# A chunked linear-attention and Mish feed-forward kernel: scores ahead of outputs in the head, three q chunks loaded in runs of eight rows, transposes and loads of the third group moved

## The chip, the cores and the metric

The kernel runs on one core of one Trainium2 chip. The metric is the device time of one execution in microseconds (us). The core has five engines with instruction queues of their own: TensorE (PE in the profile, with its weight loads as PEld), VectorE (DVE), ScalarE (ACT), GpSimd (POOL) and SyncE (SP). DMA transfers are issued from the queues of ACT, POOL and SP, and move through 16 DMA engines.

## The reference, cut to what matters

```python
# q, k, v: 4 batches, 8 heads, 768 positions, 64 columns; lam: one decay per head
Dmask = where(i >= j, lam ** (i - j), 0)
for each block of 64 positions:
    intra = ((qb @ kb.T) * Dmask) @ vb
    inter = (qb * lam ** (i + 1)) @ kv_state
    out[block] = intra + inter
    kv_state = lam ** 64 * kv_state + (kb * lam ** (63 - i)).T @ vb
x = out as 3072 tokens x 512
h = x @ w_in                                   # 512 x 2048
y = (h * tanh(softplus(h))) @ w_out            # 2048 x 512
```

## The kernel before, in words

**Tiles.** The kernel takes blocks of 128 positions (C) in place of 64, so there are 6 groups (n) of 4 batches (b), 24 chunks c = 4n + b. A chunk is one tile of q, of k and of v: 128 positions by 8 heads by 64 columns. Chunk 0 of q and k comes as float32 over the SP and ACT queues; everything else is loaded by `load_k`, `load_q` and `load_v` (lines 62 to 79) from POOL's queue, which turns float32 into float16 on the way. `chunk_rows` (line 58) puts a position on a partition, so that each of a chunk's 1024 runs is one row of 64 float32.

**The first two groups (chunks 0 to 7)** are turned with TensorE. `first_t` (line 205) transposes k and q against the identity into PSUM tiles pk and pq, four matmuls each, and copies them to SBUF as pkT (on ACT, line 219) and pqT (on DVE, line 222, or line 224 with the decays lq for chunks 4 to 7). `first_s` (line 227) makes the scores, eight matmuls into two PSUM tiles pS, and masks them on DVE into the two tiles sb (line 238; for chunks 0 to 3 the mask dm holds the decays). `first_o` (line 241) makes the outputs: eight matmuls of sb and v into pO (line 253), for chunks 4 to 7 also four of pqT and the state wst (line 249), and a copy to xt on ACT (line 255). `busy(m)` (line 163) issues m matmuls on zeros whose result nobody reads.

**State.** `scale_k` (line 260) multiplies k with its decays into ktil, on DVE for chunks 0 to 3 and 20 to 23 and on POOL for the others. `state_half` (line 281) makes half of a group's new state: 32 small matmuls pv of ktil and v (line 288), then on DVE wst (line 295, group 0) or raws (lines 301 and 303), from which POOL makes wc (line 304). `clear(b)` sets a part of wst to zero on DVE.

**Later groups.** `turn` (line 267) scales k and transposes q and k by DMA from SP's queue into qraw and kraw (line 272). `pair_s`, `pair_o` and `pair_a` work on two chunks at once: scores and state part (lines 324 and 330), outputs (line 351), state (line 288). Their output xtok goes to xt by a DMA transpose from SP (line 361).

**Dense part.** `mm1_unit` (16 for a group) and `mm1_tile` (16 for group 1) make h: ph = w_in times xt (lines 380 and 398), then Mish on ACT into hsg (lines 387 and 402). `mm2_unit` makes the result: po = hsg times w_out (line 412), copied by ACT (line 427) and stored.

**What sets the order.** Nothing is scheduled by the compiler: every engine runs its instructions in the order in which the kernel's lines issue them. The head is lines 451 to 485. Then come the loads of group 1 and of w_out on POOL's queue, the 16 units of group 0 with steps hung on unit numbers by the table `steps` (line 506), the 16 tiles of group 1 with a second table (line 524), the loads and turns of group 2 (line 533), and from line 537 the loop over the later groups, where pair steps are hung on positions of the dense list (line 553).

Of the kernel before, what the change touches and what calls it, by code (L numbers as in the profile page):

```python
# [7 lines left out]
F32 = mybir.dt.float32  # L8
F16 = mybir.dt.float16
# [11 lines left out]
def kernel(  # L21
# [39 lines left out]

    def load_k(i):
        if i == 0:
            kn[i] = const.tile([128, H, D], F32, name="kn0")
            nc.sync.dma_start(out=kn[i], in_=chunk_rows(k, i))
            return
        kn[i] = loads.tile([128, H, D], F16, name="kn", tag="kn")
        nc.gpsimd.dma_start(out=kn[i], in_=chunk_rows(k, i))  # L68

    def load_q(i):  # L70
        if i == 0:
            qn[i] = const.tile([128, H, D], F32, name="qn0")
            nc.scalar.dma_start(out=qn[i], in_=chunk_rows(q, i))
            return
# [122 lines left out]

    xt = [None] * NG
# [6 lines left out]
    def first_t(c, m=0):  # L205

        out_ = []
        first = c < B
        for src, name in ((k0 if c == 0 else kn[c] if first else ktil[c], "pk"),
                          (q0 if c == 0 else qn[c], "pq")):  # L210
# [6 lines left out]
            out_.append(work.tile([128, JP, C], F16, name=f"{name}T", tag=f"{name}T", bufs=2))  # L217
            if name == "pk":
                nc.scalar.activation(out_[-1], pt, AF.Copy)
                busy(m)  # L220
            elif first:
                nc.vector.tensor_copy(out_[-1], pt)
            else:
                nc.vector.tensor_tensor(out=out_[-1], in0=pt, in1=lq, op=ALU.mult)
        kq[c] = out_

    def first_s(c):

        kT, qT = kq[c]
# [5 lines left out]
        sb0[c] = []  # L235
        for t in range(2):
            sb0[c].append(work.tile([128, JP, C], F16, name="sb", tag="sb", bufs=4))
            nc.vector.tensor_tensor(out=sb0[c][t], in0=pS[t],  # L238
                                    in1=dm[:, t] if c < B else bc(maskT, 1, JP), op=ALU.mult)

    def first_o(c):
# [5 lines left out]
        for j in range(JP):  # L247
            if n:
                nc.tensor.matmul(psO[:, j, :], wst[:, b, j, :],
                                 kq[c][1][:, j, :], start=True, stop=False)  # L250
# [4 lines left out]
        nc.scalar.activation(xt[n][:, :, b * C : (b + 1) * C], psO, AF.Copy)  # L255
# [201 lines left out]
    first_t(0, 2)  # L457
# [5 lines left out]
    busy(1)  # L463
    first_s(0)
    first_t(1)
    clear(1)
    q_decays()
    busy(1)
    first_o(0)
    first_s(1)  # L470
    busy(3)
    first_t(2)
    clear(2)
    nc.scalar.preload_act_table(AF.Mish)
    first_o(1)
    first_s(2)
    busy(3)
    first_t(3)
    clear(3)
# [7 lines left out]
    scale_k(1)  # L487
    for i in range(B, NVB - 2):
        load_chunk(i)
# [3 lines left out]
    load_v(NVB - 2)  # L493
    load_k(NVB - 1)
    scale_k(B + 1)
# [10 lines left out]
    steps = {12: ((first_t, 4),), 14: ((first_s, 4),), 15: ((first_t, 5), (first_o, 4))}  # L506
    for u in range(NKI):
# [3 lines left out]
        if u == 1:  # L511
            scale_k(2)
            scale_k(3)
# [7 lines left out]
    c = 2 * B  # L521
    for f, i in ((load_k, c + 1), (load_q, c + 1), (load_k, c + 2), (load_q, c + 2)):
        f(i)
    steps = {(4, 0): ((first_s, 5), (first_t, 6)), (4, 1): ((first_o, 5), (first_s, 6)),
             (4, 2): ((first_t, 7),), (4, 3): ((first_o, 6), (first_s, 7)), (5, 0): ((first_o, 7),),
             (6, 1): ((state_half, 0),), (6, 2): ((state_half, 1),)}
# [5 lines left out]
    c = 2 * B  # L532
    for f, i in ((load_k, c + 3), (load_q, c + 3), (turn, c), (turn, c + 1), (load_v, c),
                 (turn, c + 2), (load_v, c + 1), (turn, c + 3), (load_v, c + 2), (load_v, c + 3)):
        f(i)

    for n in range(NT - 1, NG):
# [9 lines left out]
        if n + 1 < NG:  # L547
# [5 lines left out]
            steps = (((11, pair_s, 0), (14, pair_o, 0), (17, pair_s, 1), (20, pair_o, 1),  # L553
# [60 lines left out]
```

## Time and profile before

| | us |
|---|---|
| median of 3 runs (212.65, 213.41, 213.62) | 213.41 |
| the profiled execution, its own time | 213.85 |
| its span, first to last instruction | 212.1 |
| PE busy | 203.5 |
| POOL busy | 100.0 |
| ACT busy | 86.7 |
| DVE busy | 67.6 |
| packets of POOL's DMA queue, share of 16 engines' span | 85.2% |

In the profile a row of the timeline has the start and the length in us, then the engine, the line of the kernel, the operation, the tiles (written <- read) with shapes, and the number of instructions merged in the row; in brackets stands the idle time of the engine ahead of it and what ended it. A row's length runs to the end of its last instruction, and matmuls overlap, so the next row may start earlier. The list of waits gives for an engine and a line the idle time in all, how often, and the longest. The chain of waits is the sequence of work that ended last, each piece with its start and length. The mean granted TensorE clock is 0.999 over the span.

### The profile page before, as it was taken

The numbers are of one execution on the slowest core, as the hardware profiler recorded it, in microseconds if no ns is written. First come the engines' busy times: TensorE is split into PE (matmuls) and PEld (weight loads), VectorE is DVE, ScalarE is ACT, GpSimd is POOL, SyncE is SP. The second block draws the span as 40 slices with busy tenths as digits, with TensorE's granted clock in tenths as the row PEclk, the third lists the DMA queues.
The fourth block names the chain that finished last, engine by engine and source line by source line (L and its number), as shares of the span: only waits on it lengthen the run. The fifth ranks groups of instructions, "written<-read, shape, count | busy, mean of one in ns | idle before, by whom it ended". The sixth has DMA issues, their size and how long they took to land.

```text
span 212.1 us, 4293 instructions
## 1 busy us (share of the span) xinstructions
PE 203.5 (96%) x1758; PEld 110.5 (52%) x1758; DVE 67.6 (32%) x124; ACT 86.7 (41%) x150; POOL 100.0 (47%) x143
## 2 busy tenths in 40 slices
PE   7989898999999899999999999999999999999994
PEld 4655446999745454445554454544444544444442
DVE  7686613725004442042440042482042510000000
ACT  4764575655421112346412356312456321566120
POOL 7997389932996348786965067921000000000000
PEclk9999999999999999999999999999999999999999
DMA  9999999999999999999997799997702032100112
GB/s 129 133 157 185 189 156 99 172 189 164 121 145 195 185 182 164 163 189 153 156 166 148 182 87 84 144 166 141 190 9 49 5 99 104 49 0 0 49 53 99
DMA packets 109895, 26.78 MB, mean 126 GB/s; under 512 B 102578, under 2 KB 106930, under 8 KB 109874
## 3 DMA queue, kind: packets, MB, share of 16 engines
q0 software_dynamic: 78080, 13.37, 85.2%
q1 hardware_dynamic: 27296, 6.63, 20.4%
q10 hardware_dynamic: 4498, 6.49, 9.9%
q8 instruction: 14, 0.23, 0.5%
q14 instruction: 7, 0.06, 0.1%
HBM read 27.26 MB, written 6.29 MB: 158 GB/s over the span
## 4 chain that ended last, share of the span: by engine, by line
PE 82%; DMA 9%; DVE 2%; ACT 1%; POOL 1%; issue 1%; SPq 1%; POOLq 0%; ACTq 0%; DVEq 0%
PE po L412 33%; PE ph L380 30%; DMA kraw<-ktil 7%; PE ph L398 7%; PE pO L253 2%; PE pS L324 2%; DMA kn<-in_k_dram 2%; PE pO L351 2%; PE pS L234 1%; PE pv L288 1%; PE pk L213 1%; SPq L272 1%; PE busy L167 1%; PE pq L213 1%; POOL vz L79 1%
## 5 line engine op out<-in xcount | busy, mean ns | idle before, releaser
L412 PE MATMUL po<-wout,hsg 128*128 128x512 f16 (+2 forms) x400 | 85.4, 371 | 0.0
L380 PE MATMUL ph<-xt,win 128*128 128x512 f16 (+2 forms) x328 | 73.0, 374 | 0.5 <-ACT xt L255 0.3
L387 ACT ACTIVATE hsg<-ph 128x512 f16<-128x512 f32 x80 | 47.7, 597 | 31.4 <-PE ph L380 31.1
L412 PEld LDWEIGHTS <-hsg 128*128 128x128 f16 x400 | 37.8, 98 | 42.3
L380 PEld LDWEIGHTS <-win 128*128 128x128 f16 x328 | 30.9, 98 | 36.3 <-issue 2.0
L427 ACT ACTIVATE osb<-po 128x512 f32<-128x512 f32 (+1 forms) x24 | 14.2, 593 | 74.8 <-PE po L412 69.9
L339 DVE TENSOR_TENSOR sb<-pS,maskT 128x512 f16<-128x512 f32 x32 | 19.9, 684 | 59.6 <-PE pS L324 59.6
L68 POOL DMA_DIRECT2D kn<-in_k_dram x23 | 21.0, 913 | 4.5 <-issue 1.9
L76 POOL DMA_DIRECT2D qn<-in_q_dram x23 | 20.9, 907 | 4.6 <-DMA wout<-in_moe_w_out_dram 3.0
L79 POOL DMA_DIRECT2D vz<-in_v_dram x24 | 21.7, 908 | 2.4 <-DMA win<-in_moe_w_in_dram 1.6
L263 POOL TENSOR_TENSOR ktil<-kn,lk 128x512 f16<-128x512 f16 x16 | 16.7, 1054 | 2.5 <-DMA kn<-in_k_dram 2.3
L398 PE MATMUL ph<-xt,win 128*128 128x128 f16 x256 | 15.6, 219 | 0.7 <-ACT xt L255 0.7
L357 DVE TENSOR_TENSOR xtok<-pO,lqt 128x512 f16<-128x512 f32 x16 | 10.3, 687 | 15.5 <-PE pO L351 15.5
L398 PEld LDWEIGHTS <-win 128*128 128x128 f16 x256 | 14.5, 98 | 1.1 <-issue 0.8
L304 POOL TENSOR_TENSOR wc<-raws,lbc 128x512 f16<-128x512 f32 x8 | 8.6, 1096 | 9.8 <-DVE raws L303 5.4
L402 ACT ACTIVATE hsg<-ph 128x512 f16<-128x512 f32 x16 | 9.6, 597 | 7.5 <-PE ph L398 7.5
L421 DVE COPY osb<-po 128x128 f32<-128x128 f32 x1 | 0.3, 291 | 38.7 <-PE po L412 38.7
L368 POOL COPY tick<-hsg 1x1 f16<-1x1 f16 x25 | 4.4, 178 | 12.5 <-ACT hsg L387 12.4
L167 PE MATMUL busy<-kzero 128*128 128x512 f16 x16 | 6.6, 505 | 1.2 <-DVE kzero L149 1.2
L253 PE MATMUL pO<-sb,vz 128*128 128x128 f16 x64 | 6.4, 230 | 0.4 <-DVE sb L238 0.3
L238 DVE TENSOR_TENSOR sb<-pS,maskT 128x512 f16<-128x512 f32 x8 | 5.2, 687 | 5.1 <-PE pS L234 5.1
L263 DVE TENSOR_TENSOR ktil<-kn,lk 128x512 f16<-128x512 f16 (+1 forms) x8 | 6.5, 849 | 0.0
(71 smaller groups left out, 115.9 us busy)
## 6 DMA issues: line engine op xcount, KB each, us to landing
out_dram<-osb ACTq DMA_DIRECT2D x23, 256.0 KB, 2.6
vz<-in_v_dram POOLq DMA_DIRECT2D x24, 128.0 KB, 4.4
kn<-in_k_dram POOLq DMA_DIRECT2D x23, 128.0 KB, 5.2
qn<-in_q_dram POOLq DMA_DIRECT2D x23, 128.0 KB, 4.8
wout<-in_moe_w_out_dram POOLq DMA_DIRECT2D x4, 512.0 KB, 10.4
win<-in_moe_w_in_dram POOLq DMA_DIRECT2D x3, 512.0 KB, 9.9
kn<-in_k_dram SPq DMA_DIRECT2D x1, 256.0 KB, 3.4
qn<-in_q_dram ACTq DMA_DIRECT2D x1, 256.0 KB, 4.1
```

What stands on the lines that cost most here:

```text
L68: nc.gpsimd.dma_start(out=kn[i], in_=chunk_rows(k, i))
L76: nc.gpsimd.dma_start(out=qn[i], in_=chunk_rows(q, i))
L79: nc.gpsimd.dma_start(out=vz[i % NVB][:, :, 0:D], in_=chunk_rows(v, i))
L253: nc.tensor.matmul(psO[:, j, :], vf[:, o : o + 128], sb0[c][t][:, j, :], start=(n == 0 and t == 0), stop=(t == 1))
L263: (nc.vector if i < B or i >= (NG - 1) * B else nc.gpsimd).tensor_tensor(out=t, in0=kn[i], in1=bc(lk, 2, D), op=ALU.mult)
L339: nc.vector.tensor_tensor(out=s.sb[x][t], in0=pS[x][t], in1=bc(maskT, 1, JP), op=ALU.mult)
L357: nc.vector.tensor_tensor(out=xtok[:, :, :, t, :], in0=s.pO[t], in1=bc(bc(lqj[:, :, t], 1, 2), 3, D), op=ALU.mult)
L380: nc.tensor.matmul(ph_t[ni][:, lo:hi], win_t(ni, kc), xt[n][:, kc, lo:hi], start=(kc == 0), stop=(kc == NKC - 1))
L387: nc.scalar.activation(hsg[n][:, ni, :], ph_t.pop(ni), AF.Mish)
L398: nc.tensor.matmul(ph[:, u, :], win_t(w * s + u, kc), xt[n][:, kc, b * C : (b + 1) * C], start=(kc == 0), stop=(kc == NKC - 1),)
L412: nc.tensor.matmul(po[:, lo:hi], hsg[n][:, ki, b * C : (b + 1) * C], wout[part][:, kk, lo:hi], start=(ki == 0), stop=(ki == NKI - 1),)
L427: nc.scalar.activation(o, i, AF.Copy)
```

## The change

Five things change.

1. q of chunks 1 to 3 is loaded with eight successive rows of one head on a partition: 128 runs of 2 KB in place of 1024 of 256 bytes. Partition 16h + s then holds rows 8s to 8s + 7 of head h. `turn_pe` turns such a tile with 16 matmuls in place of 4: for each of the eight rows r and for even and odd heads, the weights are the 64 columns of row r, the moving operand is the 64 columns of the identity that pick the heads of that parity, and the result goes to every eighth float32 column of 64 partitions of pq. That tile is float32 where it was float16.
2. In the head, scores stand ahead of outputs, and the two masks of a chunk are split, so that the q copy of the next chunk stands between them. The fillers are dealt out anew (16 before and after), the clears move, and `q_decays` and the load of the Mish table move ahead.
3. `scale_k` of chunks 2 and 3 moves from behind the first half state to the end of the head, and `clear(3)` with it. On POOL `scale_k(5)` moves ahead of the load of k of chunk 7.
4. In the group 0 and group 1 parts the tables shift: chunk 4 is turned after unit 11 (was 12), scored after 13 (was 14); chunk 5 is turned after 14 (was 15) and scored after 15 (was after tile (4,0)); the outputs of chunk 7 come after tile (5,1) (was (5,0)).
5. k and q of chunk 11 are loaded ahead of the state of group 1, and chunk 8 is turned between the two halves of that state. In the loop for group 2 the pair steps stand at 9, 13, 16 and 20 (were 11, 14, 17 and 20).

```diff
     def load_q(i):
...
+        if i < B:
+            qn[i] = const.tile([128, RS, D], F16, name=f"qn{i}")
+            n, b = divmod(i, B)
+            nc.gpsimd.dma_start(
+                out=qn[i].rearrange("p r c -> p (r c)"),
+                in_=q[b, :, n * C : (n + 1) * C, :].rearrange("h (s r) c -> h s (r c)", r=RS))
             return
...
+    own = ident.rearrange("p (j x s) -> p j x s", j=JP, x=2)
...
+    def turn_pe(c, name):
+
+        src = (k0 if c == 0 else kn[c] if c < B else ktil[c]) if name == "pk" else (q0 if c == 0 else qn[c])
+        if 0 < c < B and name == "pq":
+            pt = ps.tile([128, JP, C], F32, name=name, tag=name)
+            for r in range(RS):
+                for x in range(2):
+                    nc.tensor.matmul(
+                        pt[64 * x : 64 * x + 64].rearrange("p j (s r) -> p j s r", r=RS)[:, :, :, r],
+                        src[:, r, :], own[:, :, x, :], start=True, stop=True)
+        else:
             pt = ps.tile([128, JP, C], F16, name=name, tag=name)
...
-    first_t(0, 2)
+    first_k(0)
+    busy(2)
+    first_q(0)
     clear(0)
...
-    busy(1)
-    first_s(0)
-    first_t(1)
-    clear(1)
     q_decays()
     busy(1)
-    first_o(0)
-    first_s(1)
-    busy(3)
+    scores(0)
+    masks(0, 0)
+    first_t(1)
+    masks(0, 1)
+    nc.scalar.preload_act_table(AF.Mish)
+    busy(1)
+    scores(1)
+    masks(1, 0)
+    outputs(0)
     first_t(2)
+    copy_out(0)
+    masks(1, 1)
+    busy(2)
+    first_s(2)
+    first_o(1)
+    clear(1)
+    busy(2)
+    first_t(3)
     clear(2)
-    nc.scalar.preload_act_table(AF.Mish)
-    first_o(1)
-    first_s(2)
-    busy(3)
-    first_t(3)
-    clear(3)
+    busy(2)
     first_s(3)
     first_o(2)
     busy(2)
...
     scale_k(0)
     scale_k(1)
+    clear(3)
+    scale_k(2)
+    scale_k(3)
...
-    steps = {12: ((first_t, 4),), 14: ((first_s, 4),), 15: ((first_t, 5), (first_o, 4))}
+    steps = {11: ((first_t, 4),), 13: ((first_s, 4),), 14: ((first_t, 5),), 15: ((first_o, 4), (first_s, 5))}
...
-    c = 2 * B
-    for f, i in ((load_k, c + 1), (load_q, c + 1), (load_k, c + 2), (load_q, c + 2)):
-        f(i)
+    g = 2 * B
+    for c in (g + 1, g + 2, g + 3):
+        load_k(c)
+        load_q(c)
...
+             (4, 3): ((first_o, 6), (first_s, 7)), (5, 1): ((first_o, 7),),
+             (6, 1): ((state_half, 0), (turn, g)), (6, 2): ((state_half, 1),)}
```

The rows below are the engines' own orders, from the built programs; line numbers of the changed kernel differ.

On DVE in the head, before: sb are the masked scores, pqT the copied q, wst the state tile that `clear` sets to zero, dm the mask of chunks 0 to 3. The rows start after the copy of q of chunk 0.

```order
L449 MEMSET wst 128x256
L238 TENSOR_TENSOR sb<-pS,dm 128x512 x2
L222 COPY pqT<-pq 128x512
L449 MEMSET wst 128x256
L238 TENSOR_TENSOR sb<-pS,dm 128x512 x2
L222 COPY pqT<-pq 128x512
L449 MEMSET wst 128x256
L238 TENSOR_TENSOR sb<-pS,dm 128x512 x2
L222 COPY pqT<-pq 128x512
L449 MEMSET wst 128x256
L238 TENSOR_TENSOR sb<-pS,dm 128x512 x2
```

The same stretch of DVE in the changed kernel:

```order
L490 MEMSET wst 128x256
L266 TENSOR_TENSOR sb<-pS,dm 128x512
L242 CAST pqT<-pq 128x512
L266 TENSOR_TENSOR sb<-pS,dm 128x512 x2
L242 CAST pqT<-pq 128x512
L266 TENSOR_TENSOR sb<-pS,dm 128x512 x3
L490 MEMSET wst 128x256
L242 CAST pqT<-pq 128x512
L490 MEMSET wst 128x256
L266 TENSOR_TENSOR sb<-pS,dm 128x512 x2
```

The q copy of chunk 1 stands between the two masks of chunk 0, that of chunk 2 between the two masks of chunk 1; that of chunk 3 still stands behind both masks of chunk 2. The copies are casts from float32 now, and one clear has left the stretch.

On DVE right behind, at the end of the head and in the first units, before: ktil is the scaled k, pv the raw half state.

```order
L263 TENSOR_TENSOR ktil<-kn_98,lk 128x512
L263 TENSOR_TENSOR ktil<-kn,lk 128x512
L295 TENSOR_TENSOR wst<-pv,lbc 64x8x64 x2
L263 TENSOR_TENSOR ktil<-kn,lk 128x512 x2
L295 TENSOR_TENSOR wst<-pv,lbc 64x8x64 x2
```

The same in the changed kernel:

```order
L304 TENSOR_TENSOR ktil<-kn_98,lk 128x512
L304 TENSOR_TENSOR ktil<-kn,lk 128x512
L490 MEMSET wst 128x256
L304 TENSOR_TENSOR ktil<-kn,lk 128x512 x2
L336 TENSOR_TENSOR wst<-pv,lbc 64x8x64 x4
```

All four scalings stand ahead of the first write of the state.

On POOL ahead of group 2, before: the loads of k and q of chunk 10, the two halves of the state (wc), the loads of chunk 11, and the scalings of chunks 8 to 10 with the loads of v.

```order
L68 DMA kn<-in_k_dram 128x8x64
L76 DMA qn<-in_q_dram 128x8x64
L304 TENSOR_TENSOR wc_163<-raws,lbc 128x512
L304 TENSOR_TENSOR wc_165<-raws,lbc 128x512
L68 DMA kn<-in_k_dram 128x8x64
L76 DMA qn<-in_q_dram 128x8x64
L263 TENSOR_TENSOR ktil<-kn,lk 128x512 x2
L79 DMA vz_69<-in_v_dram 128x8x64
L263 TENSOR_TENSOR ktil<-kn,lk 128x512
```

The same in the changed kernel, from the loads of chunk 10 too:

```order
L70 DMA kn<-in_k_dram 128x8x64
L85 DMA qn<-in_q_dram 128x8x64
L70 DMA kn<-in_k_dram 128x8x64
L85 DMA qn<-in_q_dram 128x8x64
L345 TENSOR_TENSOR wc_163<-raws,lbc 128x512
L304 TENSOR_TENSOR ktil<-kn,lk 128x512
L345 TENSOR_TENSOR wc_165<-raws,lbc 128x512
L304 TENSOR_TENSOR ktil<-kn,lk 128x512
L88 DMA vz_69<-in_v_dram 128x8x64
L304 TENSOR_TENSOR ktil<-kn,lk 128x512
```

The two loads of chunk 11 stand ahead of the first half state, and the scaling of chunk 8 between the halves.

80 lines of the change are left out of this document (44 added, 36 removed).

## The prediction

> **What bounds the kernel now.** I read the page's first part, then the busy time by stretches, then the list of PE's waits. The page's line of busy times:
>
> ```profile
> PE 203.5 (96%) x1758; PEld 110.5 (52%) x1758; DVE 67.6 (32%) x124; ACT 86.7 (41%) x150; POOL 100.0 (47%) x143
> ```
>
> PE is the bound nearly everywhere, and its dense products are not touched. Only PE's idle time can be won. Where it lies, the stretches show (after the length: busy us of PE, PEld, DVE, ACT, POOL, each with its count; then the granted clock, the DMA share and GB/s):
>
> ```profile
> 20.00:25.00 5.00, 4.41 (x35) 1.99 (x34) 4.51 (x10) 2.39 (x4) 1.76 (x2) 1.00 1.30 203
> 35.00:40.00 5.00, 4.44 (x80) 4.02 (x80) 2.46 (x4) 2.90 (x5) 5.00 (x7) 1.00 1.11 121
> 40.00:45.00 5.00, 4.74 (x86) 4.41 (x84) 2.69 (x5) 3.02 (x6) 3.28 (x4) 1.00 1.17 184
> ```
>
> And PE's waits, with the total, the count and the longest:
>
> ```profile
> PE ph L398 <- ACT xt L255: 0.7, 1, 0.7
> PE pS L324 <- DMA kraw<-ktil: 1.1, 2, 0.6
> PE pv L288 <- DVE ktil L263: 0.6, 2, 0.3
> PE pO L253 <- DVE sb L238: 0.3, 1, 0.3
> ```
>
> These 2.7 us are about all that edits 3 to 5 can aim at. Ahead of them lies the head, where PE is kept busy with fillers while PE, ACT and DVE pass chunks to each other; there the count of busy time says nothing, and the dependences have to be followed.
>
> **The head (edits 1 and 2).** The timeline of before:
>
> ```profile
> 7.94 1.29 DVE L238 TENSOR_TENSOR sb<-pS,dm 128x512 f16<-128x512 f32 x2 [0.47 <-PE pS L234]
> 8.19 0.63 PE L213 MATMUL pq<-ident,qn 128*128 128x128 f16 x4
> 8.62 0.63 PE L167 MATMUL busy<-kzero 128*128 128x512 f16 x1
> 10.12 0.41 PE L234 MATMUL pS<-pqT,pkT 64*128 64x128 f16 x8
> 10.46 0.82 PE L167 MATMUL busy<-kzero 128*128 128x512 f16 x3
> 11.11 0.39 PE L213 MATMUL pk<-ident,kn 128*128 128x128 f16 x4
> 11.34 0.39 PE L213 MATMUL pq<-ident,qn 128*128 128x128 f16 x4
> 14.65 0.40 PE L234 MATMUL pS<-pqT,pkT 64*128 64x128 f16 x8 [0.67 <-ACT pkT L219]
> 14.98 0.62 PE L253 MATMUL pO<-sb,vz 128*128 128x128 f16 x8
> 15.08 1.29 DVE L238 TENSOR_TENSOR sb<-pS,dm 128x512 f16<-128x512 f32 x2 [0.36 <-PE pS L234]
> 16.28 0.81 PE L380 MATMUL ph<-xt,win 128*128 128x384 f16 x4 [0.25 <-ACT xt L255]
> 18.76 0.44 PE L288 MATMUL pv<-vz,ktil 128*64 128x64 f16 x16
> ```
>
> The groups by form give the length of one DVE instruction (after the bar: busy us, mean ns):
>
> ```profile
> L238 DVE TENSOR_TENSOR sb<-pS,dm 128x512 f16<-128x512 f32 x8 | 5.2, 686 | 1.9 <-PE pS L234 1.9
> L222 DVE COPY pqT<-pq 128x512 f16<-128x512 f16 x4 | 1.7, 421 | 0.8 <-PE pq L213 0.8
> ```
>
> The unknown prices are two. The q copy becomes a cast from a float32 PSUM tile. Its floor is the old copy (0.42), its ceiling the mask, which also reads 512 float32 columns of PSUM (0.69 in length, one every 0.65 by the pair's 1.29). I take 0.65, since the mask reads the same type. The q turn becomes 16 products of 128 rows and 64 columns. The nearest row is the half state at 18.76, 16 products of that very shape: 0.44, against 0.23 between the starts of the old k and q turns (11.11 and 11.34). But those wrote neighbouring columns, the new ones write every eighth, which no row shows, so I take 0.5 and keep a high end. Below the old turn it can't be: more products of fewer columns. Early in the head PE runs at about half rate, though the granted clock reads 1.00 in the rows above: one filler took 0.63 at 8.62, where three took 0.82 at 10.46. There I take 0.8.
>
> Now the chain. The first mask ends at 8.6 as before. The q turn of chunk 1 starts at 8.2 and ends at 9.0; the cast stands ahead of the second mask, so DVE waits 0.4 and casts to 9.65; the second mask ends at 10.3. The scores of chunk 1 start at 9.7, against 10.12. Their first mask ends at 10.95. The outputs of chunk 0, now behind these scores, start at 10.35 with the second mask and take 0.45 (eight products, 14.98 to the filler behind them); the k turn, 0.23, and the q turn follow to 11.55. Cast to 12.2, second mask of chunk 1 to 12.85, masks of chunk 2 to 14.15. The outputs of chunk 1 run to 13.35, two fillers to 13.8, the turns of chunk 3 to 14.5, the cast to 15.15. So the scores of chunk 3 start at 15.2, against 14.65: what the reordering gains at chunk 1 is paid back by three slower turns and casts in series. The last mask ends as much later, near 16.9, and the first product of the dense part starts at 16.8, against 16.28. The head loses 0.5.
>
> **The half states (edit 3).** PE in the first units, and DVE beside it:
>
> ```profile
> 19.29 1.89 PE L380 MATMUL ph<-xt,win 128*128 128x512 f16 x8
> 20.74 1.29 DVE L263 TENSOR_TENSOR ktil<-kn,lk 128x512 f16<-128x512 f16 x2
> 22.09 0.32 PE L288 MATMUL pv<-vz,ktil 128*64 128x64 f16 x8 [0.29 <-DVE ktil L263]
> 22.33 7.94 PE L380 MATMUL ph<-xt,win 128*128 128x512 f16 x36
> ```
>
> One product of 512 columns comes every 0.22 (36 in 7.94). The eight of units 2 and 3 are issued by 21.05, and unit 4 starts at 22.33. Of these 1.28 us the second half state needs 0.4; 0.85 is waiting for the scalings of chunks 2 and 3, which stood on DVE behind wst. In the changed kernel DVE goes from the masks (16.9) through four scalings and a clear (4 times 0.65, and the clear under 0.3) to 19.8, ahead of the second half state at 21.6. The wait goes; wst, pushed behind, is not read before chunk 4's outputs near 34. Head and half states together: +0.5 - 0.85, that is -0.3, and unit 4 starts near 22.0.
>
> **The tables (edit 4).** PE at chunk 4's and chunk 7's outputs:
>
> ```profile
> 35.56 1.05 PE L398 MATMUL ph<-xt,win 128*128 128x128 f16 x16 [0.69 <-ACT xt L255]
> 36.55 0.40 PE L234 MATMUL pS<-pqT,pkT 64*128 64x128 f16 x8
> 42.66 1.07 PE L398 MATMUL ph<-xt,win 128*128 128x128 f16 x16
> 44.11 0.22 PE L253 MATMUL pO<-sb,vz 128*128 128x128 f16 x1 [0.26 <-DVE sb L238]
> ```
>
> Tile (4,0) waits 0.69 for the copy of the outputs just ahead of it. Now the scores of chunk 5, which cost 0.3, stand between: -0.3, and 0.35 of the wait stays. At chunk 7 the tile at 42.66 issues its last product near 43.56 (16 at 0.056), and the outputs start at 44.11: 0.55 lost. With one more tile, 0.9 long, between scores and outputs the masks are done: -0.5. Chunk 4 is turned one unit earlier, so its ktil must be there sooner. That hangs on the loads:
>
> ```profile
> 8.31 0.92 POOL L76 DMA_DIRECT2D qn<-in_q_dram  x1
> 10.91 2.30 POOL L92 DMA_DIRECT2D win<-in_moe_w_in_dram  x3
> 27.27 1.04 POOL L263 TENSOR_TENSOR ktil<-kn,lk 128x512 f16<-128x512 f16 x1 [2.35 <-DMA kn<-in_k_dram]
> 29.90 0.43 PEld L213 LDWEIGHTS <-ktil 128*128 128x128 f16 x4
> ```
>
> ktil of chunk 4 ends at 28.3, with POOL waiting for its k. PE takes it at 29.9; now at 29.9 - 0.3 - 0.87 (a unit of four products), 28.7. That still holds by 0.4, so the q loads cost and gain nothing directly. With 128 runs in place of 1024, POOL's issue should fall from 0.92 towards less than the 0.77 of a win load (2.30 for three), so three loads bring the queue forward by 0.2 each at best.
>
> **Group 2 (edit 5).** POOL, the chain of waits, and PE at the pairs:
>
> ```profile
> 55.41 2.06 POOL L263 TENSOR_TENSOR ktil<-kn,lk 128x512 f16<-128x512 f16 x2
> 64.83 8.52 DMA kraw<-ktil
> 65.90 0.62 PE L324 MATMUL pS<-qraw,kraw 64*128 64x128 f16 x16
> 73.40 0.40 PE L324 MATMUL pS<-qraw,kraw 64*128 64x128 f16 x8 [0.56 <-DMA kraw<-ktil]
> 92.75 0.40 PE L324 MATMUL pS<-qraw,kraw 64*128 64x128 f16 x8 [0.49 <-DMA kraw<-ktil]
> ```
>
> The transposes run one behind another on SP's queue from the first scaling at 55.4. With the loads of chunk 11 ahead and chunk 8's turn between the halves, that start moves to about 52 to 53, some 3 us; the second pair moves from position 17 to 16 and PE is 1.1 ahead by then, so its need comes 2 us sooner (four products are 0.87). 3 against 2 more than covers the 0.56: -0.5. The first pair, from 11 to 9, is wanted 2.8 sooner, against the 3 won. The second wait, 0.49, hangs on the output copies of the loop itself, whose distances don't change: it stays.
>
> Sum: -0.3 - 0.3 - 0.5 - 0.5 = -1.6. The profiled execution took 213.85, 1.75 of it outside the span; it would take 212.25. Against the median of 213.41 that is **211.8**.
>
> **Rules weighed.** The Trainium skill, "PSUM — Partial Sum Buffer", section Specifications (TRN2), says that PSUM has cachelines of 8 bytes and that any access pattern that is not contiguous slows matmuls significantly; the new turn writes 32 bytes apart, and no run here shows it. By it the sum would be that of the second rival or worse. The Trainium skill, "DMA: Bandwidth & Descriptors", section "Why a DMA increments its semaphore by 16 and not by 1", says that a DMA runs on the largest count up to 16 that divides the outermost sizes of both sides, with an exception for some GpSimd copies; the new q load has 8 heads outermost against 128 partitions, so eight engines. By it the third rival would hold.
>
> **The rivals.** First, the change does only half: the transposes, wanted 2 to 3 us sooner, wait again. For it: the first pair's need moves by 2.8 and its transposes by 3, so the move adds a margin of only 0.2. Against: the pair at 65.90 had no wait at all. Price 0.5 to 1.0: 212.3 to 212.8. Second, the strided turn costs twice the row or more. Every further 0.4 on a turn comes three times in series, since each cast waits for it: 0.9 a turn gives +1.2, 213.0; up to 1.3 a turn, 214.2. Third, loads on half the engines: a load is issued every 0.92 and takes at most that long of the queue, on half the engines twice that; k of chunk 4 comes up to 1.3 later when two of them share a half, ktil misses its 0.4 by 0.9: 212.7. On the other side of no change: the same strided turn where a product takes over 0.09 us in place of 0.027. At 16 products that is 1.45 a turn, three times 0.95 more, +2.85: 214.6 and slower. Against it speaks only the half state's row; it decides from 0.09 a product on.
>
> **How the numbers follow.** A difference under 0.5% (1.07 us) can't be told from none by a measurement of this kernel. Forecast 0.56, the transposes late 0.12, strided turn at two to three times 0.15, loads on half the engines 0.07, strided turn over 0.09 a product 0.10. Faster (under 212.34): most of the forecast, and the low ends of the first and third rival, 0.55. Slower (over 214.48): 0.10. Same: 0.35. The range goes from 210.8 (the cast at 0.42 saves 0.2 at two places, 0.4, and the second transpose wait goes too, 0.5) to 213.7 (strided turn near 1.1), leaving out the slow turn's tail.
>
> **What would show it.** Right: the scores of chunk 3 near 15.2; no wait of pv for ktil; a wait of about 0.35 at tile (4,0) and none at chunk 7; no wait at the second pair of group 2, the one near 92 still there, earlier by about 1.6. Wrong: a q turn over 0.7 us once PE is at full rate; a cast far from 0.65; unit 4 later than 22.4; a wait of PE for ktil of chunk 4, or of the first pair for kraw.

## The result and the profile after

| | before | changed |
|---|---|---|
| median of 9 runs each, side by side on one chip (us) | 213.41 | 212.07 |
| lowest and highest | 212.23 to 214.57 | 211.55 to 213.26 |
| ratio, with its 95% interval | | 0.9947 (0.9924 to 0.9971) |
| profiled execution, and its span | 213.85, 212.1 | 212.23, 210.4 |

The changed kernel is faster by 0.5%, with the interval on one side of no change; the interval (0.3% to 0.8%) includes the 0.5% from which the prediction counted a kernel as faster. A few runs fell into a disturbed state; medians are over all runs, ratios and verdicts over the undisturbed ones alone.

The page's line of busy times, and PE's waits (engine, tile, line, what it waited for; total, times, longest):

```profile
PE 204.0 (97%) x1794; PEld 111.0 (53%) x1794; DVE 68.3 (32%) x124; ACT 86.5 (41%) x150; POOL 98.8 (47%) x143
```

```profile
PE pS L260 <- DVE pqT L242: 0.7, 3, 0.2
PE ph L439 <- ACT xt L292: 0.4, 1, 0.4
PE ph L421 <- ACT xt L292: 0.3, 1, 0.3
```

PE has 36 more instructions, which are the three q turns at 16 in place of four. The waits for ktil, for the masks of chunk 7 and both waits for kraw are gone; 0.35 of the 0.69 for xt is left, as forecast. New are three waits for pqT, the q tile that the cast writes. The head in the timeline:

```profile
8.35 1.06 PE L222 MATMUL pq<-ident,qn 128*64 128x64 f16 x16
9.45 0.69 DVE L242 CAST pqT<-pq 128x512 f16<-128x512 f32 x1 [0.80 <-PE pq L222]
10.19 0.40 PE L260 MATMUL pS<-pqT,pkT 64*128 64x128 f16 x8 [0.24 <-DVE pqT L242]
11.18 0.39 PE L228 MATMUL pk<-ident,kn 128*128 128x128 f16 x4
11.50 0.64 PE L222 MATMUL pq<-ident,qn 128*64 128x64 f16 x16
14.65 0.64 PE L222 MATMUL pq<-ident,qn 128*64 128x64 f16 x16
16.08 0.40 PE L260 MATMUL pS<-pqT,pkT 64*128 64x128 f16 x8 [0.25 <-DVE pqT L242]
17.72 0.81 PE L421 MATMUL ph<-xt,win 128*128 128x384 f16 x4 [0.25 <-ACT xt L292]
22.92 1.25 PE L421 MATMUL ph<-xt,win 128*128 128x512 f16 x5
```

The scores of chunk 3 start at 16.08, where before had 14.65 and the forecast 15.2. PE's timeline later on, at the turn of chunk 6, group 1's half states, and the first state products of the two groups behind; first of before, then of the changed kernel:

```profile
36.88 0.40 PE L213 MATMUL pk<-ident,ktil 128*128 128x128 f16 x4
49.22 0.44 PE L288 MATMUL pv<-vz,ktil 128*64 128x64 f16 x16
80.57 0.69 PE L288 MATMUL pv<-vz,ktil 128*64 128x64 f16 x32
109.06 0.69 PE L288 MATMUL pv<-vz,ktil 128*64 128x64 f16 x32
```

```profile
37.03 0.39 PE L228 MATMUL pk<-ident,ktil 128*128 128x128 f16 x4
48.94 0.44 PE L329 MATMUL pv<-vz,ktil 128*64 128x64 f16 x16
79.55 0.70 PE L329 MATMUL pv<-vz,ktil 128*64 128x64 f16 x32
107.36 0.69 PE L329 MATMUL pv<-vz,ktil 128*64 128x64 f16 x32
```

These marks cut the program into stretches in which PE has the same work in both kernels. To the scores of chunk 3: +1.43. From there to unit 4 (22.33 and 22.92): 7.68 and 6.84, -0.84. To the turn of chunk 6: 14.55 and 14.11, -0.44. To the half states: 12.34 and 11.91, -0.43. To the states of the next group: 31.35 and 30.61, -0.74. To those of the one after: 28.49 and 27.81, -0.68. The sum is -1.70, and nothing differs behind. So the total came out as forecast (-1.6), but two terms did not: the head cost 0.9 more, and a wait that was to stay, 0.49 near 92, went. (The two waits for kraw, 0.56 and 0.49 in their rows, cost their stretches 0.74 and 0.68: matmuls overlap, so a row counts its wait from the end of the product ahead, 0.18 to 0.19 after the next one would have started.)

### The profile page after: what moved, and what is told of

It reads as the page before. It is cut to its first block, busy times and chain, and to the rows that moved or that the text cites. A ratio compares the mean times of both kernels' runs of the same rounds, so it can differ in the third digit from the quotient of the medians.

```text
span 210.4 us, 4359 instructions
## 1 busy us (share of the span) xinstructions
PE 204.0 (97%) x1794; PEld 111.0 (53%) x1794; DVE 68.3 (32%) x124; ACT 86.5 (41%) x150; POOL 98.8 (47%) x143
## 4 chain that ended last, share of the span: by engine, by line
PE 94%; DMA 2%; DVE 1%; ACT 1%; issue 0%
PE po L453 40%; PE ph L421 34%; PE ph L439 7%; PE pS L365 2%; PE pO L286 2%; PE pO L392 2%; DMA kn<-in_k_dram 2%; PE pv L329 1%; PE pS L260 1%; DVE pqT L242 1%; PE pk L228 1%; PE pq L222 1%; PE pO L371 1%; PE pq L228 1%; PE busy L176 1%; ACT xt L292 1%
## 5 line engine op out<-in xcount | busy, mean ns | idle before, releaser
L85 POOL DMA_DIRECT2D qn<-in_q_dram x20 | 18.0, 898 | 5.5 <-DMA wout<-in_moe_w_out_dram 4.2
L292 ACT ACTIVATE xt<-pO 128x512 f16<-128x512 f32 x8 | 4.8, 596 | 4.6 <-PE pO L286 4.4
```

The lines of the kernel that those rows point to most:

```text
L85: nc.gpsimd.dma_start(out=qn[i], in_=chunk_rows(q, i))
```

## The experiments

The theory: edit 1 costs the head most of what the other edits gain, since its turn writes every eighth column and its cast stands in series; edits 3 to 5 gain what the stretches show. The rivals: the reordering costs the head; the loads by runs are what lets the rest go early; the waits for kraw come and go by themselves.

All profiled executions in the same stretches (us; "scores" is the start of the scores of chunk 3; then the stretches to unit 4, to the turn of chunk 6, to the half states of group 1, and to the state products of the two groups behind):

| kernel | scores | unit 4 | chunk 6 | half states | states | next states | span |
|---|---|---|---|---|---|---|---|
| before | 14.65 | 7.68 | 14.55 | 12.34 | 31.35 | 28.49 | 212.1 |
| before, second execution | 14.19 | 7.77 | 14.54 | 12.35 | 31.06 | 27.80 | 210.7 |
| before with edit 5 | 14.65 | 7.69 | 14.54 | 12.35 | 30.61 | 27.81 | 210.7 |
| changed | 16.08 | 6.84 | 14.11 | 11.91 | 30.61 | 27.81 | 210.4 |
| changed, second | 15.17 | 6.84 | 14.11 | 11.91 | 31.93 | 27.80 | 210.8 |
| changed, third | 15.33 | 6.84 | 14.11 | 11.91 | 31.38 | 27.80 | 210.5 |
| turn writes contiguously | 14.68 | 6.84 | 14.11 | 11.91 | 30.61 | 27.81 | 209.0 |
| turn reads contiguously | 16.01 | 6.84 | 14.10 | 11.91 | 30.62 | 27.81 | 210.4 |
| edits 3 to 5 | 14.38 | 7.12 | 14.32 | 11.91 | 30.62 | 27.83 | 209.2 |
| edits 2 to 5 | 13.91 | 6.84 | 14.30 | 11.91 | 30.62 | 27.80 | 208.4 |
| edits 2 to 5, second | 13.60 | 7.70 | 14.35 | 11.91 | 30.89 | 27.80 | 209.3 |
| edits 2 to 5, pair at 17 | 13.66 | 7.61 | 14.35 | 11.90 | 30.62 | 27.80 | 209.0 |
| edits 2 to 5, two more moves | 14.19 | 7.99 | 13.90 | 11.91 | 30.68 | 27.83 | 209.6 |

Behind the head, a stretch in which PE waits for engines alone comes back within 0.02 from execution to execution; where a DMA is waited for, it moves by up to 1.3. The head itself moves by up to 0.9 in one kernel. No run undoes edit 3 or edit 4 alone: what they gain is read from these stretches.

**Edit 1 undone.** In `load_q` and `turn_pe`:

```diff
-            qn[i] = const.tile([128, RS, D], F16, name=f"qn{i}")
...
+            qn[i] = const.tile([128, H, D], F16, name=f"qn{i}")
+            nc.gpsimd.dma_start(out=qn[i], in_=chunk_rows(q, i))
...
-        if 0 < c < B and name == "pq":
+        if False:
```

> The changed kernel with edit 1 alone undone: q of chunks 1 to 3 comes in 1024 rows and is turned by four transposes of 128 columns; the reordered head, the tables and group 2 stay. Theory (the row runs are what the head paid with): the turn falls from 0.64 to about 0.25, the cast from 0.69 to 0.42, three times in series, so the scores of chunk 3 start near 14.8 in place of 16.08 and the first dense product near 16.5 in place of 17.72; POOL's q loads take 0.9 again, ktil of chunk 4 ends near 28.3 and PE wants it near 28.6, so nothing is lost there: 210.9. Rival one (the casts and masks in series on DVE, not the turn, set the head): scores of chunk 3 at 15.6 or later, 211.7. Rival two (the loads by runs were needed): the head is as much earlier as the theory says, but PE waits 0.5 or more for the keys of chunk 4, 211.5 to 212.

Measured: 0.9927 of before (0.9893 to 0.9962), span 208.4. Its head, and the first use of chunk 4's scaled keys:

```profile
10.46 0.39 PE L225 MATMUL pq<-ident,qn 128*128 128x128 f16 x4
10.88 0.43 DVE L239 COPY pqT<-pq 128x512 f16<-128x512 f16 x1 [0.49 <-PE pq L225]
13.91 0.40 PE L257 MATMUL pS<-pqT,pkT 64*128 64x128 f16 x8
15.54 0.81 PE L418 MATMUL ph<-xt,win 128*128 128x384 f16 x4 [0.25 <-ACT xt L289]
27.85 0.23 PEld L225 LDWEIGHTS <-ktil 128*128 128x128 f16 x4 [0.52 <-POOL ktil L301]
```

The head is shorter by more than the theory had: counted from the scores of chunk 0 (7.26 there, 7.16 here), the scores of chunk 3 come 6.75 later in place of 8.82, that is 2.07. This is one pair of executions; over all of them the distance is 7.98 to 8.82 with edit 1 (the two kernels of the same head, the changed one and the contiguous read) and 6.45 to 6.75 without (the kernel with two more moves, which waits for q, left out), so edit 1 costs the head 1.2 to 2.4. The part that stays is the one from the scores of chunk 1 to those of chunk 3, 5.88 to 5.89 with and 4.66 to 4.74 without. The profiled execution of this kernel was also the fastest of its eleven runs. Rival one falls by its number; how much of the cost is the cast, follows below. Of rival two something holds: PE's weight load now waits for ktil of chunk 4, and the stretch to chunk 6 is 0.19 longer (14.30 for 14.11). The loads explain it, POOL's rows first of the changed kernel, then of this one:

```profile
7.84 0.64 POOL L80 DMA_DIRECT2D qn<-in_q_dram  x1
26.38 1.04 POOL L304 TENSOR_TENSOR ktil<-kn,lk 128x512 f16<-128x512 f16 x1 [2.38 <-ACT hsg L428]
```

```profile
8.31 0.92 POOL L79 DMA_DIRECT2D qn<-in_q_dram  x1
26.75 1.04 POOL L301 TENSOR_TENSOR ktil<-kn,lk 128x512 f16<-128x512 f16 x1 [2.37 <-ACT hsg L425]
```

A load by runs is issued in 0.64 in place of 0.92, and ktil of chunk 4 ends at 27.42 in place of 27.79. What it saves is POOL's time, not time on the way: from the issue to the landing the three q loads took 5.1, 5.0 and 4.7 in the changed kernel and 4.1, 4.2 and 4.2 here (over all executions 4.4 to 5.2 by runs of eight rows, 4.1 to 5.0 by single rows).

**The turn's write, and its read.** Once each product writes 64 neighbouring columns, once it reads 64 neighbouring columns of the identity; the outputs that come out otherwise for it are those of chunks 1 to 3.

```diff
-                        pt[64 * x : 64 * x + 64].rearrange("p j (s r) -> p j s r", r=RS)[:, :, :, r],
+                        pt[64 * x : 64 * x + 64].rearrange("p j c -> p (j c)")[:, 64 * r : 64 * r + 64],
```

```diff
-                        src[:, r, :], own[:, :, x, :], start=True, stop=True)
+                        src[:, r, :], ident[:, 64 * x : 64 * x + 64], start=True, stop=True)
```

> The changed kernel where each of the 16 products of a q turn writes 64 neighbouring columns in place of every eighth one (the columns of q of chunks 1 to 3 come out in another order, so their outputs are others; loads, number of products, casts are the same). Theory (writing PSUM every 32 bytes is what makes the turn slow): two products every 32 ns in place of 56, the turn 0.45 in place of 0.64, scores of chunk 3 near 15.5 in place of 16.08, 211.5. Rival one (the read of the identity in pieces of 16 columns is what makes it slow): the turn stays at 0.64 and the time at 212.1. Rival two (the write is slow, but the chain goes over DVE's casts and masks): the turn at 0.45, the scores of chunk 3 within 0.2 of 16.08, 212.

> The changed kernel where the 16 products of a q turn read 64 neighbouring columns of the identity in place of four pieces of 16 (so they place other elements; the outputs of chunks 0 of each batch row beyond the first are others), writing every eighth column as before. Theory (the write is slow): the turn stays at 0.64, 56 ns for two products. Rival (the read is slow): the turn at about 0.45, 32 ns for two.

Measured: the contiguous write gave 0.9905 of before (0.987 to 0.994) and a span of 209.0, the contiguous read a span of 210.4 in its one run. The 16 products of chunk 2's turn, in the view by tile (shortest, median and longest in ns; first and last start in us), for the changed kernel, the contiguous write and the contiguous read:

```profile
L222 PE MATMUL pq<-ident,qn x16: 243/247/247, 11.5 to 11.9; 128*64 128x64 f16 x16
```

```profile
L222 PE MATMUL pq<-ident,qn x16: 196/196/217, 10.5 to 10.7; 128*64 128x64 f16 x16
```

```profile
L222 PE MATMUL pq<-ident,qn x16: 243/247/247, 11.4 to 11.8; 128*64 128x64 f16 x16
```

The write is the cause, the read costs nothing. The turns as one row each of the timeline, of the contiguous write, then of the contiguous read:

```profile
10.49 0.44 PE L222 MATMUL pq<-ident,qn 128*64 128x64 f16 x16
14.68 0.40 PE L260 MATMUL pS<-pqT,pkT 64*128 64x128 f16 x8 [0.25 <-DVE pqT L242]
```

```profile
11.43 0.64 PE L222 MATMUL pq<-ident,qn 128*64 128x64 f16 x16
16.01 0.40 PE L260 MATMUL pS<-pqT,pkT 64*128 64x128 f16 x8 [0.25 <-DVE pqT L242]
```

The turn takes 0.44 as the half state of that shape did, against 0.64: 0.20 for 16 products. From the scores of chunk 1 to those of chunk 3, two turns further, it is 5.89 in the changed kernel (10.19 to 16.08), 5.49 with the contiguous write (9.19 to 14.68) and 4.66 with edit 1 undone (9.25 to 13.91). So each turn at full rate pays 0.20 for the write and 0.41 for the rest of edit 1: the cast of 0.69 against the copy's 0.43, the largest part; a gap of about 0.08 more ahead of the turn; and 16 products in place of four, 0.44 to the end of the last against 0.39. Of the 1.40 by which the scores of chunk 3 came earlier here, 0.40 are these two turns, 0.14 an earlier start, and 0.86 lie at chunk 1, where the write isn't the only cause: in this execution PE reached full rate about 2 us sooner (below). Against the changed kernel's second execution (below), whose first turn ran at full rate too, the scores of chunk 3 are 0.49 earlier (14.68 for 15.17), and 0.40 of it are these two turns.

**Edits 1 and 2 undone**, with the scalings ahead of the half states, the tables and group 2 kept; the head is that of before, without `clear(3)`, and q is loaded and turned as above.

```diff
-    scores(0)
-    masks(0, 0)
+    first_s(0)
     first_t(1)
-    masks(0, 1)
...
-    scores(1)
-    masks(1, 0)
-    outputs(0)
+    first_o(0)
+    first_s(1)
+    busy(3)
     first_t(2)
```

> The changed kernel with edits 1 and 2 undone: q of chunks 1 to 3 in 1024 rows and the head in the order of before (outputs ahead of scores, both masks together), with the scalings of chunks 2 and 3 ahead of the half states, the tables and group 2 kept. Theory (edits 1 and 2 together cost the head 1.4): scores of chunk 3 at 14.65, first dense product near 16.3, unit 4 near 21.5, and 210.7, if PE doesn't wait for the keys of chunk 4 (ktil at 28.3, wanted near 28.4). Between this and the kernel that undoes edit 1 alone lies the price of the reordering: if that one is earlier than this one, edit 2 gains by itself; if it is the same within 0.3, it does nothing. Rival (the reordering is what lets the half states run early): unit 4 at 22 or later, 211.3 or more.

Measured: 0.9918 of before (0.9884 to 0.9952), span 209.2. The head:

```profile
14.38 0.40 PE L257 MATMUL pS<-pqT,pkT 64*128 64x128 f16 x8 [0.67 <-ACT pkT L234]
16.01 0.81 PE L418 MATMUL ph<-xt,win 128*128 128x384 f16 x4 [0.25 <-ACT xt L289]
17.54 1.27 PE L418 MATMUL ph<-xt,win 128*128 128x384 f16 x12 [0.27 <-DMA win<-in_moe_w_in_dram]
```

Against the kernel with edits 2 to 5 the scores of chunk 3 are 0.47 later (14.38 to 13.91, with chunk 0's at 7.16 in both): the reordering gains 0.47 by itself, where edit 1 loses 2.07. Again this is one pair: from the scores of chunk 0 to those of chunk 3 the four executions with outputs first take 7.04 to 7.50, the three with scores first and without edit 1 take 6.45 to 6.75, so the gain has its sign in each and its size not. The half states run without a wait in this head too, so the rival falls. What the shorter head arrives at, shows in the last row: PE waits for columns of the input weights.

**The same kernels again, with two more.** On another chip the changed kernel, the one with edit 1 undone, one with two more moves, and before with edit 5 alone:

```diff
     first_o(1)
-    clear(1)
-    busy(2)
     first_t(3)
+    clear(1)
...
-    steps = {11: ((first_t, 4),), 13: ((first_s, 4),), 14: ((first_t, 5),), 15: ((first_o, 4), (first_s, 5))}
+    steps = {11: ((first_t, 4),), 13: ((first_s, 4),), 14: ((first_t, 5), (first_o, 4)), 15: ((first_s, 5),)}
```

> The changed kernel once more, as the measure for the other kernels of this set on the same chip. All theories: a span near 210.4 and a time near 212.1, the scores of chunk 3 near 16.0, no wait of PE for kraw near 91. How far its median is from its first one (212.07) is what a median of this kernel moves from chip to chip.

> The changed kernel with edit 1 undone, once more. Theory (edit 1 costs 2.1 us of the head and buys nothing that PE waits for later): span 208.4, time 2 us below that of the changed kernel of this set. Rival (the early load is worth something in some executions, since PE takes the keys of chunk 4 only 0.1 after they are scaled): a wait of PE for ktil or for the queries of chunk 6 of 0.3 to 1 us shows up in this execution, and the gain against the changed kernel is 1 us or less.

> The changed kernel with edit 1 undone and two more moves: the two fillers and the clear ahead of chunk 3's turn go (both clears behind its cast), and the outputs of chunk 4 stand ahead of unit 15 in place of behind it, so that the copy of them is done by tile (4,0). Theory: the scores of chunk 3 near 13.6 in place of 13.9, first dense product near 15.2, and the wait of 0.35 at tile (4,0) gone for at most 0.15 of waiting at the outputs: span 207.8, time 0.5 below the kernel that only undoes edit 1. Rival (the loads bind once the head is this short): PE waits 0.3 to 0.5 for the first columns of the input weights or for the scaled keys of chunk 4, and the time is within 0.3 of that kernel. If this rival holds, it also says what the row runs of edit 1, which bring the queue forward by 0.7, could be worth.

> The kernel before with edit 5 alone. Theory (edit 5 alone takes both waits for kraw): no wait of PE for kraw, neither at the second pair of group 2 nor near 92; the half states' wait of 0.85 and the 0.69 at tile (4,0) stay; span 212.1 - 0.56 - 0.49, that is 211.0, time 212.8. Rival (the second wait hangs on the output copies of the loop, as the prediction had it): the second wait of 0.4 to 0.5 is still there, span 211.5.

Measured, against before at 213.4: the changed kernel 211.89, 0.9937 (0.991 to 0.9964); edit 1 undone 211.15, 0.9911 (0.9876 to 0.9945); two more moves 211.58, 0.992 (0.9889 to 0.995); edit 5 alone 212.58, 0.996 (0.9939 to 0.998). The profiled execution of the last is no measure: its span is 728.6 us, and PE starts a product of 128 columns every 0.21 there, in place of 0.056, though the granted clock reads 1.00; its nine other runs lie at 212.0 to 212.9. The changed kernel was not what its expectation said:

```profile
7.86 0.64 PE L222 MATMUL pq<-ident,qn 128*64 128x64 f16 x16
15.17 0.40 PE L260 MATMUL pS<-pqT,pkT 64*128 64x128 f16 x8 [0.25 <-DVE pqT L242]
71.92 0.40 PE L365 MATMUL pS<-qraw,kraw 64*128 64x128 f16 x8 [1.14 <-DMA kraw<-ktil]
```

Its head was 0.9 shorter, since the first q turn already ran at full rate (0.64 for 1.06), and the second pair of group 2 waited 1.14 for kraw. With edit 1 undone the loads now held PE up, in the first dense stretch; the kernel with the two moves shows the same, and waits for q in the head:

```profile
17.03 1.27 PE L418 MATMUL ph<-xt,win 128*128 128x384 f16 x12 [0.54 <-DMA win<-in_moe_w_in_dram]
```

```profile
10.70 0.40 PE L225 MATMUL pq<-ident,qn 128*128 128x128 f16 x4 [0.35 <-DMA qn<-in_q_dram]
22.18 3.19 PE L418 MATMUL ph<-xt,win 128*128 128x512 f16 x14 [1.02 <-DMA win<-in_moe_w_in_dram]
```

So both rivals held in the main: the shorter head meets the queue of loads and gives back up to 1.15 (the stretch to unit 4, 7.61 to 7.99 for 6.84, in three of four executions). The waits are for columns of the input weights, longer than the rival had them, and the kernel with the two moves came out 0.43 above the one that only undoes edit 1, not within 0.3. The head's length alone doesn't decide it, since the execution without such a wait has its scores of chunk 3 at 13.91 and the one with the longest at 14.19. The loads themselves move: they are issued alike up to 17.9, but the first one that POOL holds back until a load of the input weights is in starts at 20.92 in the execution without a wait, and at 21.54, 21.51 and 22.42 in the three others (20.55 to 20.87 in the changed kernel). The two moves gained their 0.4 at tile (4,0) (13.90 for 14.30) and lost it at the loads.

**The waits themselves.** Before, the changed kernel and before with edit 5 once more for their profiles, and edit 1 undone with the second pair of group 2 where it was:

```diff
-            steps = (((9, pair_s, 0), (13, pair_o, 0), (16, pair_s, 1), (20, pair_o, 1),
+            steps = (((9, pair_s, 0), (13, pair_o, 0), (17, pair_s, 1), (20, pair_o, 1),
```

> The kernel before once more, for its waits alone. Theory (the waits for kraw come from how far the transposes have got when PE arrives, and that moves from execution to execution): at least one of the two waits, 0.56 at the second pair of group 2 and 0.49 near 92, differs from its first value by 0.3 or more, while the waits on engines (0.69 at tile (4,0), the half states' 0.3 and 0.3, 0.26 at chunk 7) stay within 0.05. Rival (both waits are set by the order of the program): both come back within 0.15.

> The changed kernel a third time, for its waits alone. Its first execution had no wait for kraw, its second one of 1.14 at the second pair of group 2, with the scores of chunk 3 at 16.08 and at 15.17. Theory (the transposes run on their own clock, so what PE gains ahead of them is waited for at the pair): if the scores of chunk 3 come near 15.2 again, the second pair waits 0.5 to 1.2; if they come near 16, it waits under 0.3; the span is within 0.5 of 210.6 in both cases. Rival (the wait of 1.14 was a single late transfer): no wait, and the span follows the head.

> The kernel before with edit 5 alone, for its waits (the first profile of it is of an execution of 728 us and shows nothing of this). Theory (edit 5 alone takes both waits): no wait for kraw at the second pair of group 2 nor near 92; the half states' 0.3 and 0.3 and the 0.69 at tile (4,0) stay; span 211.0. Rival (the second wait hangs on the output copies, as the prediction had it): 0.4 to 0.5 near 92, span 211.5.

> The changed kernel with edit 1 undone and the second pair of group 2 back at position 17, as before, in place of 16. Theory (with the shorter head PE comes to the second pair 2 us sooner than its transposes were planned for, and waits there in some executions): the pair is wanted 0.87 later, its wait is gone, and the median is 0.2 to 0.5 below that of the kernel that only undoes edit 1 (0.9911 of before), that is 0.987 to 0.990 of before. Rival (the pair's position does nothing, the gain is lost at the input weights' columns): 0.991 to 0.993 of before, and PE's waits are for win.

Measured. Before, at the second pair of group 2 and at the first of group 3:

```profile
72.73 0.40 PE L324 MATMUL pS<-qraw,kraw 64*128 64x128 f16 x8 [0.26 <-DMA kraw<-ktil]
91.18 0.62 PE L324 MATMUL pS<-qraw,kraw 64*128 64x128 f16 x16
```

The changed kernel at the second pair, and before with edit 5 at the same two places:

```profile
71.53 0.40 PE L365 MATMUL pS<-qraw,kraw 64*128 64x128 f16 x8 [0.59 <-DMA kraw<-ktil]
```

```profile
71.58 0.62 PE L324 MATMUL pS<-qraw,kraw 64*128 64x128 f16 x16
91.12 0.62 PE L324 MATMUL pS<-qraw,kraw 64*128 64x128 f16 x16
```

The wait near 92 is there in one execution of before and in none of the twelve others of the table: it belonged to that execution, not to the order. The wait at the second pair was 0.56 and 0.26 in before, and 0, 1.14 and 0.59 in the changed kernel. In its three executions it was long where the head was short, as the theory says; but with the contiguous write (half states at 47.5) and with edit 1 undone (47.0 and 47.5) PE came as early or earlier and waited 0 to 0.3. So an early PE alone doesn't make the wait; the transposes' own arrival moves as much. The last transpose of the group, in the three executions of the changed kernel:

```profile
62.45 1.30 SPq L313 DMA_TRANSPOSE kraw<-ktil  x1
```

```profile
63.14 2.01 SPq L313 DMA_TRANSPOSE kraw<-ktil  x1
```

```profile
62.99 2.28 SPq L313 DMA_TRANSPOSE kraw<-ktil  x1
```

From this issue to its landing it took 5.8, 8.7 and 8.5, which gives the waits of 0, 1.14 and 0.59. In before (issued at 64.83 and 64.47) it took 8.5 and 8.2, with edit 5 alone 5.9, and 5.8 to 7.9 in the other kernels. The issue moves by 0.7 within one kernel, the landing by 2.9.

Edit 1 undone with the pair at 17 gave 211.04, 0.9881 of before (0.9834 to 0.9928), the lowest ratio of all. Its profile has no wait for kraw, but waits for win:

```profile
15.59 0.82 PE L418 MATMUL ph<-xt,win 128*128 128x384 f16 x4 [0.55 <-DMA win<-in_moe_w_in_dram]
70.74 0.62 PE L362 MATMUL pS<-qraw,kraw 64*128 64x128 f16 x16
```

Against edit 1 undone alone (0.9911) the intervals overlap; that the position gains is not shown.

## Why the prediction came out right, and where it was wrong

**The time.** 211.8 was forecast, 212.07 measured. The sum of the profiled execution, -1.6, came as -1.70, but as +1.43 - 0.84 - 0.87 - 0.74 - 0.68, where the forecast had +0.5 - 0.85 - 0.8 - 0.5 - 0. That the sums agree so well is luck: 0.9 too little for the head is made up by 0.68 for a wait that only this execution of before had, and by 0.24 in the wait ahead of it. Over the three executions of the changed kernel and the two of before the spans average 210.6 and 211.4, 0.8 apart; the timed medians are 1.34 apart here and 1.51 in the second set. So the forecast had the direction and about the size, but not the hundredths that the sum suggests. Two details of its text don't come out: the rows that it calls on for the granted clock lie at 20 us and later (at 8 to 9 it reads 1.00 too, see the last section), and the ends of its range add up to 210.9 and 213.6.

**The head (edits 1 and 2): mis-sized by 0.9 in the profiled execution.** The step that failed is the price of the q turn, "so I take 0.5", and early "There I take 0.8". It was 0.64 at full rate and 1.06 early. In the chain: the turn of chunk 1 started 0.15 later than worked out and took 0.26 longer, which with the cast behind it put the scores of chunk 1 at 10.19 for 9.7. From there to the scores of chunk 3 it was 5.89 for 5.5: two more turns at +0.14 each, and about 0.1 more ahead of each. The cast took 0.69, the length of the mask, for the 0.65 taken. The 0.4 of the two later turns came back in all three executions (5.88 to 5.89). The 0.5 at chunk 1 did not: in the other two the first turn ran at full rate, the scores of chunk 1 stood at 9.28 and 9.45, and those of chunk 3 at 15.17 and 15.33, near the 15.2 that was named. That is luck too, since there the early turn, priced too high, made up for the later ones, priced too low. Against before (14.65 and 14.19) the head lost 0.5 to 1.9, according to when PE reached full rate. That "what the reordering gains at chunk 1 is paid back by three slower turns" was right in kind: 0.47 gained and 2.07 paid in the first pairs of executions. The second rival is this mechanism; it was priced from twice the row on, and the truth is 1.45 times the row (0.64 to 0.44). The Trainium skill, "PSUM — Partial Sum Buffer", section Specifications (TRN2), says that patterns that are not contiguous slow matmuls; the trace agrees for this write, by 0.20 in 0.44, and the read in four pieces cost nothing.

**The half states (edit 3): right.** -0.85 forecast, -0.84 measured, and 6.84 in every execution in which no load stood in between. Unit 4 was later than 22.4, the mark named as a sign of error, in the first execution alone (22.92, then 22.01 and 22.17), because of the head.

**The tables (edit 4): right.** -0.3 and -0.5 forecast, -0.44 and -0.43 measured, the same in all executions of the changed kernel. The wait of 0.35 that was to stay at tile (4,0) stayed.

**Group 2 (edit 5): half right.** The first wait: edit 5 alone makes the stretch 30.61, against 31.35 and 31.06 in before, so it gains 0.45 to 0.74. But the first rival, transposes late again, held in two of three executions of the changed kernel, at 0.59 and 1.14; a margin of some 0.2 to 1, worked out from one execution, is smaller than what the arrival of the transposes moves by. The step that failed is "3 against 2 more than covers the 0.56": the first scaling did start 2 to 3 earlier (52.44 to 52.88, for 55.41 and 55.03 in before), but the last transpose was issued only 1.3 to 2.4 earlier, its landing moves by 2.9, and PE came 0.8 to 2.1 earlier (the pair's first products at 71.29, 70.38 and 70.54, for 72.44 and 72.07). That the wait was gone in the first execution is luck: its last transpose landed after 5.8. The second wait: "it stays" failed. It was taken for a property of the loop from its one occurrence.

**The loads: right in this kernel, and incomplete.** That they "cost and gain nothing directly" holds in all three executions of the changed kernel, in which ktil of chunk 4 was done well ahead (27.42, wanted at 29.84). The third rival, a load slower by half the engines, fell in what it was to cost: no engine waited for a load by runs, and ktil came earlier, not later. What the prediction didn't see is that the long head hides the loads: with edit 1 undone PE's weight load waits for ktil in every execution, and PE for win in three of four. What earlier loads would be worth there, up to 1.15, is an estimate from those waits. The kernel whose turn writes contiguously has the loads by runs and a head 1.4 shorter, and in its one profiled execution shows neither wait.

**Edit 1 in sum.** In the profiled executions it costs 1.1 to 2.4 of the span (210.4 to 210.8 against 208.4 to 209.3), in the timed runs 0.74 (211.89 against 211.15 on the same chip) or 0.4 (0.9947 against 0.9927, on two chips), with overlapping intervals both times. So the timed runs alone don't show that it costs, and the profiles do, with a size that moves. By the profiles, all of what the change gains is in edits 2 to 5, and without edit 1 and with the pair at 17 it reaches 0.9881. What the row runs would be worth with a turn that writes contiguously, so that the columns come out in order by the choice of what is read, was not tried.

## What to carry to other kernels

Cost a matmul by the pattern it writes, not only by its shape: the same 16 products were 0.44 into neighbouring columns and 0.64 into every eighth, and in a chain of turns and casts that was paid three times. Behind the head, stretches that wait for engines alone came back within 0.02; a wait on a DMA seen once is one draw, and a term for it needs a second execution or a range, and so does a head in which PE's rate changes. And before shortening a stretch, look for what is just in time behind it: here the loads took back up to 1.15 of what the shorter head had won.

## What the runs showed of the hardware

PE reaches full rate at a moment that moves between executions. The same products at the same place tell it: the first q turn takes 1.06 at 8.35 in one execution of the changed kernel and 0.64 at 7.86 in the next, while the granted clock reads 1.00 in both; here are the two stretches (length; busy us of PE, PEld, DVE, ACT, POOL with counts; granted clock, DMA share, GB/s), the first execution, then the second:

```profile
8.00:9.00 1.00, 1.00 (x18) 0.81 (x18) 0.65 (x1) 0.81 (x2) 1.00 (x2) 1.00 1.66 150
```

```profile
7.00:8.00 1.00, 0.91 (x19) 0.70 (x20) 0.71 (x3) 1.00 (x5) 1.00 (x2) 1.00 2.11 149
```

Over the executions the last slow product lies between 7.2 and 10.1, and the scores of chunk 3 move by 0.9 with it in the changed kernel and by 0.46 in before. The Trainium skill, "TensorE: Matmul & The Clock Gate", Part 1, says that PE runs at half rate until a free-running window of activity of about 3.4 us has passed, and that the number of cold products therefore differs from run to run; the trace agrees in both (in before a filler every 0.43 early and every 0.22 later, and the spread just given), without showing the window itself. The granted clock of the profile doesn't tell the rate: it reads 1.00 through the slow products here, and 1.00 in the execution of 728.6 us. What sets the moment of full rate, and what delays the landing of a transpose by 2.9 us in one execution and not in the next, stays open.
